# Loads of v on two DMA queues, and three quarters of the E-times-v products summed in f32 before TensorE

## The chip, the core and the metric

The kernel runs on one core of a Trainium2 chip. The metric is device time in microseconds (us): 225.95 us is the median of three runs of the kernel before (225.94 to 226.25). The changed kernel is timed in the same way.

## What is computed

The input x (`A_x`) has 2048 rows of 512 numbers in bf16. After a layernorm it goes through an attention branch and, beside it, through a gated feed-forward branch; their product is added to x:

```python
xn = layernorm(x)
# attention: 32 heads of 16; each position sees w = 0..7, that is position s - 2*w
q, k, v = split(xn @ wqkv)
logits = einsum("bhsd,bhswd->bhsw", q, k[s - 2*w]) * 16 ** -0.5      # s - 2*w < 0 is masked
o = einsum("bhsw,bhswd->bhsd", softmax(logits), v[s - 2*w])
s = o @ wo
# feed-forward
h = gelu_tanh(xn @ w_gate) * (xn @ w_up)                              # 1792 wide
g = silu(h @ w_down)
out = x + s * g
```

## The kernel before

The rows are worked in four chunks of 512 (j = 0 to 3). For each chunk the program issues, in this order:

1. `glu(j, fc)` for fc = 0 to 13 (line 459): eight matmuls give a gate and an up tile in PSUM; ScalarE applies gelu to one (`ge`, line 465) and copies the other (`u`, line 467); VectorE multiplies them into `h` (line 469).
2. `qkv(j + 1, fo)`, twelve projections for the next chunk, each four matmuls and a copy on ScalarE into q, k or v. v goes to DRAM (`vT`, line 290).
3. `down(j, 0)` (14 matmuls into `y_ps`, then silu); then `sums(j)` (line 530); then `down(j, 1..3)`.
4. `divide(j)` (line 449) on VectorE, then `finish(j, 0..3)` (line 488): four matmuls with `wo` into `s_ps`, a product `m` and a sum `o_t` on VectorE, a store.

In chunk 3 there is no next chunk, and `sums(3)` stands before glu fc 12.

Every engine works through its instructions in the order in which the program issues them. What belongs to the attention is put between the stages by hand: `at((stage, j, i), fn, ...)` (line 509) hangs a function on a place, and `run` (line 512) issues it there, ahead of that step's own instructions.

The attention of chunk j lies on VectorE and TensorE:

- `qk_products` (line 320): products of q with k shifted by 2w, 16 instructions, issued in the qkv stage of the chunk before.
- `logits` (line 339): 32 matmuls with a 0/1 matrix sum the products over a head's 16 numbers; ScalarE takes the exponential into `E`. It stands inside `sums` of the chunk before.
- `load_v` (line 300): the array `va` has 128 partitions: partition 32*wl + h holds head h, shifted by 2*wl, with 16 rows of 520 columns. Four DMAs, one for each wl, read it from `vT`. Each fills 32 partitions with 512 runs of 1040 bytes.
- The products of E and v over the four groups g of 4 of the 16 rows, in one of two forms. `av_product` (line 401) takes one group and one half wh of the window: one bf16 product of 2048 columns, twice per group. `av_pair` (line 412) takes one row d of a group and both halves: one product with a result in f32 (`two`), then a sum of the two halves into bf16. It takes four such pairs of instructions for a group, and TensorE then has half as much to sum.
- `av_sums` (line 432): matmuls with 32 output columns sum the products over wl: 4 for each group in the pair form, 8 in the other. [...]

`sums(j)` issues `denominators(j)`, `av_sums(j)`, `logits(j + 1)`, `reciprocals(j)` (VectorE, line 385), the store of the reciprocals to DRAM (line 389), the four loads that spread them (`rb`, line 395), and at last `load_v(j + 1)`. All DMAs are issued by SyncE's queue (SP), in this order.

Buffers that matter: the PSUM pool `mm` has four buffers which are handed out in turn to `g_ps`, `u_ps`, `qkv_ps`, `y_ps`, `s_ps` and the logits; so the first `g_ps` of a chunk takes the buffer of the first `s_ps` of the chunk before, and has to wait until its `m` is done. `ge` and `u` have three buffers each. `va` has one buffer, and half of the next chunk's q-k products (`pk4`) share it.

The loop that sets the places before:

```python
if j + 1 < NJ:
    npair, whole, pairs = 2, (0, 7, 12, 13), (1, 2, 3, 5, 6, 8, 10, 11)
else:
    npair, whole, pairs = 1, (0, 1, 3, 5, 7, 9), (2, 4, 6, 8)
```

`npair` groups are in the pair form; `pairs` and `whole` name the glu steps at which the instructions stand. Chunk 0 has all its groups in the whole form.

Of the kernel before, what the change touches and what calls it, by code (L numbers as in the profile page):

```python
# [18 lines left out]
WL = 4  # L19
# [9 lines left out]
def kernel(  # L29
# [13 lines left out]
    nc = tc.nc  # L43
    B, S, D = A_x.shape
    DF = B_w_gate.shape[1]
    NT, NC, NF, NJ = S // P, D // P, DF // P, S // TQ
# [222 lines left out]
    st = [dict(pk={}, pv={}, vst={}) for _ in range(NJ)]  # L269
# [25 lines left out]
    def qkv(j, fo):  # L295
        ps = mm.tile([P, 1, TQ], F32, name="qkv_ps", tag="mm")
        project(ps[:, 0, :], wqkv_sb, fo * P, j)
        copy_out(j, fo, ps[:])

    def load_v(j, wls=range(WL)):  # L300

        if wls[0] == 0:
            st[j]["va"] = vap.tile([P, DH, VW], BF16, name="v_arr", tag="va")
        va = st[j]["va"]
        for wl in wls:
            nc.sync.dma_start(
                out=va[H * wl : H * (wl + 1), :, :],
                in_=bass.AP(
                    tensor=vT.tensor,
                    offset=PAD + j * TQ - WL * DIL - DIL * wl,  # L310
                    ap=[[SV * DH, H], [SV, DH], [1, VW]],
                ),
            )
# [25 lines left out]
    def logits(j):  # L339
        if j == 0:  # L340
            nc.scalar.preload_act_table(AF.Exp)
            quad = att.tile([P, NC, TQ], F32, name="L_ps", tag="quad")
            L = [quad[:, wh, :] for wh in range(WH)]
        else:
            L = [mm.tile([P, TQ], F32, name="L_ps", tag="mm")[:] for _ in range(WH)]

        Eb = st[j]["Eb"] = ep.tile([P, WH, TQ], BF16, name="E")
        E = st[j]["E"] = Eb[:, ::-1, :]
        for wh in range(WH):
            for c in range(NC):  # L350
                for wl in range(WL):
                    nc.tensor.matmul(  # L352
                        L[wh][H * wl : H * (wl + 1), :],
                        lhsT=dsum[:, c, :],
                        rhs=st[j]["pk"][WL * wh + wl][:, c, :],
                        start=(c == 0),
                        stop=(c == NC - 1),
                    )
        for wh in range(WH):
            nc.scalar.activation(out=E[:, wh, :], in_=L[wh], func=AF.Exp, scale=SCALE)  # L360
        if j == 0:
            for w in range(1, W):
                wh, wl = divmod(w, WL)
                nc.gpsimd.memset(E[H * wl : H * (wl + 1), wh, 0 : w * DIL], 0.0)

    def denominators(j):

        E = st[j]["E"]
        den = mm.tile([P, P], F32, name="den_ps", tag="mm")
        for wh in range(WH):  # L370
            for q in range(4):
                nc.tensor.matmul(  # L372
                    den[H * q : H * (q + 1), :],
                    lhsT=hsum[:],
                    rhs=E[:, wh, q * P : (q + 1) * P],
                    start=(wh == 0),
                    stop=(wh == WH - 1),
                )
        st[j]["den"] = den

    def reciprocals(j):
        den = st[j]["den"]
        rs = sm2.tile([P, P], BF16, name="rs")
        with nc.allow_low_precision(reason="as the softmax of the reference"):
            nc.vector.reciprocal(out=rs[:], in_=den[:])
        st[j]["rs"] = rs

    def store_reciprocals(j):
        nc.sync.dma_start(out=rs_d[j][:, :], in_=st[j]["rs"][:])

    def spread_reciprocals(j):

        rb = op.tile([P, TQ], BF16, name="rb")
        for i in range(WL):
            nc.sync.dma_start(
                out=rb[H * i : H * (i + 1), :].rearrange("h (q i) -> h q i", q=4),
                in_=rs_d[j].rearrange("(q h) i -> h q i", h=H),
            )
        st[j]["rb"] = rb
# [32 lines left out]
    def av_sums(j):  # L432

        o = att.tile([P, NC, TQ], F32, name="o_ps", tag="quad")
        for g in range(NC):
            pv = st[j]["pv"]
            pvs = [pv[g]] if g in pv else [pv[g, wh] for wh in range(WH)]
            for n, p in enumerate(pvs):
                for i in range(4):
                    nc.tensor.matmul(  # L440
                        o[H * i : H * (i + 1), g, :],
                        lhsT=hsum[:],
                        rhs=p[:, i, :],
                        start=(n == 0),
                        stop=(n == len(pvs) - 1),
                    )
        st[j]["o"] = o
# [40 lines left out]
    def finish(j, tt, cols, sl):  # L488

        t, n = j * TPQ + tt, cols.stop - cols.start  # L490
        s = mm.tile([P, n], F32, name="s_ps", tag="mm")
        for g in range(NC):
            nc.tensor.matmul(  # L493
                s[:],
                lhsT=st[j]["oT"][:, g, tt * P : (tt + 1) * P],
                rhs=wo_sb[:, g, cols],
                start=(g == 0),
                stop=(g == NC - 1),
            )
        m = sm2.tile([P, n], BF16, name="m")  # L500
        nc.vector.tensor_tensor(out=m[:], in0=s[:], in1=sl[:], op=ALU.mult)  # L501
        o_t = sm4.tile([P, n], BF16, name="o_t")
        nc.vector.tensor_tensor(out=o_t[:], in0=m[:], in1=x_sb[:, t, cols], op=ALU.add)
        nc.sync.dma_start(out=out2d[t * P : (t + 1) * P, cols], in_=o_t[:])
# [4 lines left out]
    def at(key, fn, *args):  # L509
        side.setdefault(key, []).append((fn, args))  # L510

    def run(stage, j, i):
        for fn, args in side.get((stage, j, i), ()):
            fn(*args)
# [15 lines left out]
    def sums(j):  # L530

        if j + 1 < NJ:
            nc.scalar.preload_act_table(AF.Exp)
        denominators(j)
        av_sums(j)
        if j + 1 < NJ:
            logits(j + 1)
        reciprocals(j)
        store_reciprocals(j)
        spread_reciprocals(j)  # L540
        if j + 1 < NJ:
            load_v(j + 1)

    for j in range(1, NJ):
        at(("qkv", j, 2), k_halo, j)
        for i in range(2):
            at(("qkv", j, 4 + 4 * i), qk_products, j, range(W), 2 * i, 2)

        if j + 1 < NJ:
            npair, whole, pairs = 2, (0, 7, 12, 13), (1, 2, 3, 5, 6, 8, 10, 11)  # L550
        else:
            npair, whole, pairs = 1, (0, 1, 3, 5, 7, 9), (2, 4, 6, 8)
        for i, fc in enumerate(pairs):
            at(("glu", j, fc), av_pair, j, i // 4, i % 4)
        for i, fc in enumerate(whole):
            at(("glu", j, fc), av_product, j, npair + i // 2, i % 2)
    at(("glu", NJ - 1, 12), sums, NJ - 1)

# [3 lines left out]
    pairs = [(8 + 2 * i, mm.tile([P, 2, HQ], F32, name="v_ps", tag="mm")[:]) for i in range(2)]  # L564
# [65 lines left out]
    for n, fo in enumerate((0, 2, 4, 6, 8, 10)):  # L630
# [5 lines left out]
                project(ps[:, i, i0 : i0 + w], wqkv_sb, (fo + i) * P, 0, HQ + i0, w)  # L636
        copy_out(0, fo, ps[:], HQ, HQ, 2)
    at(("glu", 0, 0), transpose_by_dma, TPQ)
    at(("glu", 0, 0), load_v, 0)
    for t in range(TPQ + 1, 2 * TPQ):  # L640
        at(("glu", 0, 0), transpose_by_dma, t)
    at(("glu", 0, 0), load_late_weights)
# [2 lines left out]
    for j in range(NJ):  # L645
        for fc in range(NF):
            run("glu", j, fc)
            glu(j, fc)
        if j + 1 < NJ:

            for i, fo in enumerate((0, 1, 4, 5, 2, 3, 6, 7, 8, 9, 10, 11)):
                run("qkv", j + 1, i)
                qkv(j + 1, fo)
            full = slice(0, D)
            sl = []
            for tt in range(TPQ):
                run("down", j, tt)
                sl.append(down(j, tt, full))
                if tt == 0:
                    sums(j)  # L660
            divide(j)
            for tt in range(TPQ):
                finish(j, tt, full, sl[tt])
        else:
            full, half = slice(0, D), (slice(0, D - P), slice(D - P, D))
            sl = [down(j, tt, full) for tt in range(TPQ - 1)]
            divide(j)
            finish(j, 0, full, sl[0])
            finish(j, 1, full, sl[1])
            finish(j, 2, full, sl[2])  # L670
            sl3 = down(j, 3, half[0])
            finish(j, 3, half[0], sl3)
            sl3 = down(j, 3, half[1])
            finish(j, 3, half[1], sl3)
# [28 lines left out]
```

The softmax here doesn't subtract the row's maximum and nothing guards it: scores larger than these inputs give would overflow.

## Time and profile before

| what | value |
|---|---|
| median of three runs | 225.95 us (225.94 to 226.25) |
| the profiled execution | 226.18 us, of which the span of the profile is 224.5 us |
| TensorE matmul busy | 219.3 us |
| VectorE busy | 172.9 us |
| ScalarE busy | 130.8 us |
| DMA queue | 24.66 MB, 47.1% of 16 engines' span |

The stages of chunk 1 and the start of chunk 2, in us from the span's start, with the busy time of three engines in each stretch:

| stretch | stage | length | TensorE | VectorE | ScalarE |
|---|---|---|---|---|---|
| 72.9 to 97.1 | glu of chunk 1 | 24.20 | 24.09 | 22.36 | 17.08 |
| 97.1 to 107.4 | qkv of chunk 2 | 10.30 | 10.25 | 9.58 | 7.17 |
| 107.4 to 122.9 | down of chunk 1, with the sums | 15.50 | 15.45 | 11.74 | 7.43 |
| 122.9 to 126.3 | finish of chunk 1 | 3.40 | 3.35 | 2.38 | 0.60 |

A chunk thus takes 53.4 us, and the granted clock of TensorE is 1.00 in all of these stretches. In the lines of a profile, a name such as `pv<-E,v_arr` reads "written from"; what stands in brackets at the end of a line of the timeline is the idle time just before it and what ended it.

### The profile page before, as it was taken

What the parts mean: (1) busy time and instruction counts of PE and PEld (TensorE: products, weight loads), DVE (VectorE), ACT (ScalarE), POOL (GpSimd) and SP (SyncE); (2) the same over time, 40 slices, a digit from 0 to 9 for tenths busy, and PEclk for the clock granted to TensorE, in tenths of its full rate; (3) what the DMA queues carried; (4) which work ended last, traced back from release to release, by engine and by line L of the source; (5) the groups of instructions that cost most, each with busy time, mean ns of one, the idle gap of its engine ahead of it and who ended that gap; (6) DMA issues with size and microseconds to landing.
All of it is one profiled execution on the core that took longest, in us unless ns stands there. A gap on an engine that the chain in (4) does not pass through costs nothing.

```text
span 224.5 us, 3548 instructions
## 1 busy us (share of the span) xinstructions
PE 219.3 (98%) x1293; PEld 106.0 (47%) x1314; DVE 172.9 (77%) x295; ACT 130.8 (58%) x207; POOL 21.6 (10%) x67
## 2 busy tenths in 40 slices
PE   8999999999999999999999999999999999999994
PEld 4994444444444444444444444444444444444443
DVE  4688963999984799989984799998944389982452
ACT  4386779667631767676752386767763177666211
POOL 1025981000120000000040000000000000000000
PEclk9999999999999999999999999999999999999999
DMA  6999799972079910000219960000117960001002
GB/s 207 376 402 260 148 198 146 359 212 96 12 152 199 213 23 0 0 3 1 93 41 210 187 164 0 3 0 0 67 41 151 197 147 0 0 0 28 6 23 70
DMA packets 30258, 24.89 MB, mean 111 GB/s; under 512 B 11040, under 2 KB 29728, under 8 KB 30240
## 3 DMA queue, kind: packets, MB, share of 16 engines
q1 hardware_dynamic: 30240, 24.66, 47.1%
q8 instruction: 10, 0.16, 0.3%
q14 instruction: 8, 0.07, 0.1%
HBM read 18.74 MB, written 4.34 MB: 103 GB/s over the span
## 4 chain that ended last, share of the span: by engine, by line
PE 96%; ACT 1%; issue 1%; DVE 0%; ACTq 0%
PE u_ps L261 22%; PE y_ps L477 22%; PE g_ps L261 20%; PE qkv_ps L261 16%; PE s_ps L493 6%; PE L_ps L352 3%; PE o_ps L440 3%; PE qk_ps L576 2%; ACT u L467 1%; PE warm_ps L244 1%; PE v_ps L576 1%; PE qk_ps L567 1%; PE den_ps L372 0%; PE v_ps L567 0%; PE trb L220 0%
## 5 line engine op out<-in xcount | busy, mean ns | idle before, releaser
L261 PE MATMUL u_ps<-xnT,wu_sb 128*128 128x512 bf16 x221 | 57.3, 379 | 0.4
L261 PE MATMUL g_ps<-xnT,wg_sb 128*128 128x512 bf16 x217 | 56.3, 379 | 0.1
L477 PE MATMUL y_ps<-wd_sb,h 128*128 128x512 bf16 (+2 forms) x234 | 49.5, 366 | 0.2
L467 ACT ACTIVATE u<-u_ps 128x512 bf16<-128x512 f32 x56 | 33.5, 599 | 14.8 <-PE u_ps L261 14.8
L465 ACT ACTIVATE ge<-g_ps 128x512 bf16<-128x512 f32 x56 | 33.5, 598 | 11.9 <-PE g_ps L261 8.9
L332 DVE TENSOR_TENSOR pk<-q_sb,k_sb 128x1024 bf16<-128x1024 bf16 (+1 forms) x56 | 38.9, 761 | 1.7 <-ACT k_sb L285 1.7
L261 PE MATMUL qkv_ps<-xnT,wqkv_sb 128*128 128x512 bf16 (+2 forms) x197 | 36.8, 344 | 0.2
L477 PEld LDWEIGHTS <-h 128*128 128x128 bf16 x238 | 22.6, 98 | 26.5 <-issue 1.3
L261 PEld LDWEIGHTS <-wu_sb 128*128 128x128 bf16 x224 | 21.9, 98 | 26.4
L261 PEld LDWEIGHTS <-wg_sb 128*128 128x128 bf16 x224 | 21.7, 98 | 26.6 <-issue 0.8
L404 DVE TENSOR_TENSOR pv<-E,v_arr 128x2048 bf16<-128x2048 bf16 x22 | 26.7, 1220 | 7.4 <-DMA v_arr<-vT 7.4
L485 ACT ACTIVATE sl<-y_ps 128x512 bf16<-128x512 f32 (+2 forms) x17 | 9.7, 572 | 32.7 <-PE y_ps L477 31.6
L469 DVE TENSOR_TENSOR h<-ge,u 128x512 bf16<-128x512 bf16 x56 | 23.1, 419 | 5.9 <-ACT u L467 5.8
L261 PEld LDWEIGHTS <-wqkv_sb 128*128 128x128 bf16 x200 | 18.9, 98 | 17.4
L501 DVE TENSOR_TENSOR m<-s_ps,sl 128x512 bf16<-128x512 f32 (+2 forms) x17 | 11.1, 655 | 18.4 <-PE s_ps L493 13.5
L420 DVE TENSOR_TENSOR two<-E,v_arr 128x1024 f32<-128x1024 bf16 x20 | 24.4, 1218 | 0.0
L204 POOL TENSOR_TENSOR rstd<-rstd,mhalf 128x1 f32<-128x1 f32 x12 | 7.0, 583 | 90.3 <-DVE rstd L201 90.3
L452 DVE TENSOR_TENSOR oT<-o_ps,rb 128x1024 bf16<-128x1024 f32 x8 | 9.4, 1217 | 7.7 <-DMA rb<-rs_d 7.7
L493 PE MATMUL s_ps<-wo_sb,oT 128*128 128x512 bf16 (+2 forms) x64 | 14.6, 366 | 0.2
L428 DVE TENSOR_TENSOR pv<-two 128x512 bf16<-128x512 f32 x20 | 13.8, 692 | 0.7
L465 ACT ACT_TABLE_LOAD x4 | 5.1, 1283 | 11.3 <-PE g_ps L261 11.3
L285 ACT ACTIVATE vst<-qkv_ps 128x512 bf16<-128x512 f32 x14 | 8.4, 597 | 3.7 <-PE qkv_ps L261 3.7
(65 smaller groups left out, 145.2 us busy)
## 6 DMA issues: line engine op xcount, KB each, us to landing
v_arr<-vT SPq DMA_DIRECT2D x16, 520.0 KB, 8.5
vT<-vst SPq DMA_DIRECT2D x8, 256.0 KB, 2.4
out_dram<-o_t SPq DMA_DIRECT2D x15, 128.0 KB, 3.4
wg_sb<-in_B_w_gate_dram SPq DMA_DIRECT2D x2, 896.0 KB, 9.9
wu_sb<-in_B_w_up_dram SPq DMA_DIRECT2D x2, 896.0 KB, 11.2
wd_sb<-in_B_w_down_dram SPq DMA_DIRECT2D x1, 1792.0 KB, 11.6
wqkv_sb<-in_A_wqkv_dram SPq DMA_DIRECT2D x4, 384.0 KB, 4.4
x_sb<-in_A_x_dram SPq DMA_DIRECT2D x3, 512.0 KB, 7.8
```

The costliest lines, as they stand in the source:

```text
L261: nc.tensor.matmul(ps, lhsT=w[:, dk, lo : lo + P], rhs=xnT[j][:, dk, i0 : i0 + n], start=(dk == 0), stop=(dk == NC - 1),)
L332: nc.vector.tensor_tensor(out=st[j]["pk"][w][:, c0 : c0 + n, :], in0=st[j]["q"][:, c0 : c0 + n, :], in1=k_sb[j][:, c0 : c0 + n, off : off ...
L404: nc.vector.tensor_tensor(out=pv[:], in0=st[j]["E"][:, wh, :].unsqueeze(1).to_broadcast([P, 4, TQ]), in1=st[j]["va"][:, 4 * g : 4 * g + 4, ...
L420: nc.vector.tensor_tensor(out=two[:], in0=st[j]["Eb"][:], in1=bass.AP(tensor=v.tensor, offset=v.offset, ap=[v.ap[0], [WL * DIL, WH], [1, T ...
L428: nc.vector.tensor_tensor(out=st[j]["pv"][g][:, d, :], in0=two[:, 0, :], in1=two[:, 1, :], op=ALU.add)
L465: nc.scalar.activation(out=ge[:], in_=g_ps[:], func=AF.Gelu_apprx_tanh)
L467: nc.scalar.activation(out=u[:], in_=u_ps[:], func=AF.Copy)
L469: nc.vector.tensor_tensor(out=h[:], in0=ge[:], in1=u[:], op=ALU.mult)
L477: nc.tensor.matmul(y[:], lhsT=st[j][fc][:, tt * P : (tt + 1) * P], rhs=wd_sb[:, fc, cols], start=(fc == 0), stop=(fc == NF - 1),)
L485: nc.scalar.activation(out=sl[:], in_=y[:], func=AF.Silu)
L493: nc.tensor.matmul(s[:], lhsT=st[j]["oT"][:, g, tt * P : (tt + 1) * P], rhs=wo_sb[:, g, cols], start=(g == 0), stop=(g == NC - 1),)
L501: nc.vector.tensor_tensor(out=m[:], in0=s[:], in1=sl[:], op=ALU.mult)
```

## The change

Three things change.

1. `load_v` takes a queue. The loads of wl 0 and 1 (partitions 0 to 63) stay on SyncE's queue, those of wl 2 and 3 (partitions 64 to 127) are issued by ScalarE's queue. In `sums` they stand on ScalarE behind the two exponentials; for chunk 0 they stand at glu step 4.
2. In chunks 1 and 2 three groups of four take the pair form (two before), in chunk 3 two (one before).
3. The places move: the first `av_pair` of chunk j stands at the start of `finish(j - 1, 0)`, that is on VectorE between the `divide` and the first `m`; in chunks 1 and 2 the last two pairs stand at the first step of the qkv stage; and `sums(3)` stands before glu fc 13 and not 12.

```diff
-    def load_v(j, wls=range(WL)):
-
-        if wls[0] == 0:
+    def load_v(j, wls, queue):
+
+        if "va" not in st[j]:
             st[j]["va"] = vap.tile([P, DH, VW], BF16, name="v_arr", tag="va")
         va = st[j]["va"]
         for wl in wls:
-            nc.sync.dma_start(
+            queue.dma_start(
...
         if j + 1 < NJ:
-            load_v(j + 1)
+
+            load_v(j + 1, (0, 1), nc.sync)
+            load_v(j + 1, (2, 3), nc.scalar)
...
         if j + 1 < NJ:
-            npair, whole, pairs = 2, (0, 7, 12, 13), (1, 2, 3, 5, 6, 8, 10, 11)
+            npair, whole, pairs = 3, (4, 9), (0, 1, 2, 3, 6, 7, 8, 11, 12, 14, 14)
         else:
-            npair, whole, pairs = 1, (0, 1, 3, 5, 7, 9), (2, 4, 6, 8)
+            npair, whole, pairs = 2, (3, 6, 9, 11), (0, 1, 2, 4, 5, 7, 8)
+        at(("finish", j - 1, 0), av_pair, j, 0, 0)
         for i, fc in enumerate(pairs):
-            at(("glu", j, fc), av_pair, j, i // 4, i % 4)
+            key = ("glu", j, fc) if fc < NF else ("qkv", j + 1, 0)
+            at(key, av_pair, j, (i + 1) // 4, (i + 1) % 4)
         for i, fc in enumerate(whole):
             at(("glu", j, fc), av_product, j, npair + i // 2, i % 2)
-    at(("glu", NJ - 1, 12), sums, NJ - 1)
+    at(("glu", NJ - 1, 13), sums, NJ - 1)
...
-    at(("glu", 0, 0), load_v, 0)
+    at(("glu", 0, 0), load_v, 0, (0, 1), nc.sync)
+    at(("glu", 0, 4), load_v, 0, (2, 3), nc.scalar)
...
             for tt in range(TPQ):
+                run("finish", j, tt)
                 finish(j, tt, full, sl[tt])
```

## The prediction

> **What bounds the kernel now.** I read the page's busy times first, then the chain of waits, then VectorE's and SyncE's timelines over one chunk, then the DMA lines of the v loads.
>
> ```profile
> PE 219.3 (98%) x1293; PEld 106.0 (47%) x1314; DVE 172.9 (77%) x295; ACT 130.8 (58%) x207; POOL 21.6 (10%) x67
> ```
>
> TensorE is busy for 219.3 of 224.5 us: it hardly ever waits. Only matmuls taken away can shorten the time, and any new wait of TensorE adds to it. The chain has the sums of products that the change touches:
>
> ```profile
> 110.69 1.29 PE o_ps L440 x24
> ```
>
> 24 of them take 1.29 us, 54 ns each. The instructions on VectorE, from the groups by line:
>
> ```profile
> L404 DVE TENSOR_TENSOR pv<-E,v_arr 128x2048 bf16<-128x2048 bf16 x22 | 26.7, 1220 | 7.4 <-DMA v_arr<-vT 7.4
> L420 DVE TENSOR_TENSOR two<-E,v_arr 128x1024 f32<-128x1024 bf16 x20 | 24.4, 1218 | 0.0
> L428 DVE TENSOR_TENSOR pv<-two 128x512 bf16<-128x512 f32 x20 | 13.8, 692 | 0.7
> ```
>
> VectorE's timeline around the end of chunk 1 (start, length, instruction, idle time before and who ended it):
>
> ```profile
> 110.85 0.95 DVE L385 RECIPROCAL rs<-den_ps 128x128 bf16<-128x128 f32 x1
> ...
> 117.78 2.36 DVE L452 TENSOR_TENSOR oT<-o_ps,rb 128x1024 bf16<-128x1024 f32 x2 [0.72 <-DMA rb<-rs_d]
> 123.86 0.69 DVE L501 TENSOR_TENSOR m<-s_ps,sl 128x512 bf16<-128x512 f32 x1 [3.72 <-PE s_ps L493]
> ...
> 129.44 1.23 DVE L404 TENSOR_TENSOR pv<-E,v_arr 128x2048 bf16<-128x2048 bf16 x1 [1.26 <-DMA v_arr<-vT]
> ```
>
> See that VectorE has a hole of 3.72 us ahead of the first `m`, and that v lands only at 129.44, 5.6 us after that `m`. The queue that issues the loads:
>
> ```profile
> 111.82 0.33 SPq L389 DMA_DIRECT2D rs_d<-rs  x1
> 113.30 2.66 SPq L395 DMA_DIRECT2D rb<-rs_d  x4
> 116.14 2.70 SPq L306 DMA_DIRECT2D v_arr<-vT  x4
> ```
>
> The first v load goes out 4.34 us after the reciprocal has ended (111.80). In the other chunks this step is 3.41 us (58.90 to 62.31) and 3.87 us (165.22 to 169.09). The second and fourth load of chunk 2, each looked up alone, land so many us after their own issue (last column):
>
> ```profile
> v_arr<-vT SPq DMA_DIRECT2D x1, 520.0 KB, 7.3
> v_arr<-vT SPq DMA_DIRECT2D x1, 520.0 KB, 11.2
> ```
>
> The second is issued 0.68 us after the first, so half of v is there 8.0 us after the first issue (8.2 and 8.1 us in the other chunks), all of it after 13.3.
>
> [...] bandwidth from 65 to 78 us, 40 slices:
>
> ```profile
> GB/s 243 208 176 176 186 195 189 198 195 195 173 202 182 246 234 214 198 202 202 176 233 189 186 170 179 198 179 181 181 191 158 59 20 42 359 394 369 397 278 281
> ```
>
> It stays near 190, rises to 246 at 69.2 us, 1.3 us before the second load lands (70.5), where the queue passes from partition 63 to 64, and is 359 to 397 for rows over all 128 partitions. So both halves side by side should take about half as long. [...] No run here shows two issuers[...]. [...]
>
> **The change part by part.**
>
> *TensorE.* Each of chunks 1, 2 and 3 loses four sums: 12 x 54 ns = 0.65 us less.
>
> *VectorE.* A group changes from 2 x 1.14 us (start to next start) to four pairs of 1.86 us (77.74 to 79.00 and 0.60 more): 7.44 - 2.28 = 5.2 us more a chunk. With its `h`, a pair takes 2.20 us (79.94 to 82.14) and a whole one 1.475 us (184.02 to 185.49); an `h` alone 0.34. The glu stage of chunks 1 and 2 gets 9 x 2.20 + 2 x 1.475 + 3 x 0.34 = 23.8 us (24.2 before, 129.44 to 153.6), the qkv stage 2 x 1.86 = 3.7 us, the hole before `m` 1.86 us.
>
> *ScalarE.* Two issues at 0.66 us (2.65 us for four on SP) = 1.3 us, behind the exponentials. Those end at 60.94, the next silu waits for TensorE with 1.21 us to spare, and its PSUM buffer is wanted four tiles later: cost 0, and 0 up to 3 us. In chunk 0 they stand at about 24.7 us, v being stored by 22.57 (when SP went on): gelu is late by 1.3 us where two PSUM tiles allow 1.7. What is behind them, gelu and the copies, loses no more: 0.
>
> *The new wait.* The first pair of chunk j needs all of v and stands ahead of `m`. Behind it are the four `m`, and TensorE's next four PSUM tiles wait for those. Before, the last `m` ended at 74.30 and its buffer was wanted at 75.34; less 0.1 for the signal there is 0.95 us of room. And a late reciprocal makes the wait longer, as SP issues wl 0 and 1 behind `rb`. That closes a loop on VectorE, from one reciprocal's end to the next:
>
> - to the first v issue 3.9 us (mean of the three above);
> - to the landing of SP's half 8.0 us. ScalarE's half starts earlier (114.4 in chunk 2) and is not last;
> - first pair 1.86; four `m` and `o_t` 4 x 1.06 = 4.24 (123.86 to 124.92);
> - glu 23.8; two pairs 3.7; sixteen q-k products 9.67 (9.72 to the reciprocal's place); reciprocal 0.95.
>
> The sum is 56.1 us. Before, the same loop was 4.34 + 13.3 + 24.2 + 9.65 + 0.95 = 52.4 us, and 0.97 us of waiting for k made it TensorE's 53.4. Now it is longer than TensorE's period of 53.4 - 0.2, and VectorE with its DMAs sets the pace over the chunk ends.
>
> The times: chunk 0's v lands at 30.6 (SP, 22.57 + 8.0) and 32.7 (ScalarE, 24.7 + 8.0), before VectorE wants it at 33.8, so its 3.75 us of waiting goes and the products q-k start when k is copied, 47.3 in place of 48.31. First reciprocal: 58.90 - 0.9 = 58.0. The next ones: 114.1 and 170.2. The first `m` comes 3.9 + 8.0 + 1.86 = 13.76 us later: 71.8, 127.9, 184.0, against 70.43, 123.86, 177.28 before. After the third, TensorE is late by 184.0 - 177.28 - 0.95 = 5.8 us (0.4 at the first end, then about 2.7 at each; the savings of chunks 1 and 2 are in it).
>
> *Chunk 3.* VectorE leaves the last `o_t` at 188.2; up to the product at step 11 it has 7 x 2.20 + 3 x 1.475 + 0.34 + 1.14 = 21.3 us: 209.5. TensorE enters the glu at 179.76 + 5.8, and 13 steps of 1.73 us, 0.23 and 20 sums later (209.3) it wants that product: 0.4 us of waiting, less 0.2 saved. The later reciprocal (about 211.2) gives `oT` at 211.2 + 6.1 + 2.4 = 219.7; TensorE's three downs last to 220.6: covered.
>
> Sum: 5.8 + 0.4 - 0.2 = 6.0 us on the profiled execution's 226.18, that is 232.2, and 232.0 on the median of 225.95.
>
> *Unknown costs.* The issue step: 3.4 to 4.3 us. SP's landing: [...] up to 9.2 if both streams hinder each other or `rb` and its store. Each us of the two together counts three times: 3.9 + 8.0 give 232, 11.0 together 229, 13.5 together 237. I take the measured values, since nothing in the trace says which way sharing goes.
>
> **Rivals.**
>
> - *The cover holds, faster.* If issue and landing together take at most 10.0 us (two us less, over three ends, cancels the 5.8), no `m` is late and the 0.65 us remain: 225.3. For it: VectorE's hole is 3.7 us wide and the pair 1.86. Against it: SP's half alone needs 8.0.
> - *No bandwidth is gained.* [...] all 2048 runs take their 12 us from ScalarE's first: 60.94 + 1.2 + 12 + 1.3 = 75.4, first `m` at 77.3, 5.9 us too late, and about as much at each end, since the loads follow the exponentials: 3 x 5.8 + 0.2 = 17.6, that is 243.5. [...] against it: the step to 246.
> - *Half the lateness.* Between 10.0 and 11.0 us together: 225.5 to 228.5.
>
> **Numbers.** About 0.2% (0.45 us) can be told from no change here. Likeliest, 228.5 to 237: 0.72. Half: 0.08. Cover holds: 0.11. No bandwidth: 0.06. Over 237 otherwise: 0.03. The range 226.5 to 237.5 takes in the likeliest and most of the half. Faster 0.11, same 0.03, slower 0.86.
>
> **What would show it.** SP's half landing 8 us after its first issue and bandwidth over 300 GB/s; VectorE idle about 4 us on v ahead of a first pair; `g_ps` waiting for `m` at the chunk ends, most at the second and third; reciprocals 56 us apart; 96 sums in place of 108. I am wrong if reciprocals stay 53.4 us apart, or if v is there before VectorE leaves `divide`.

## The result and the profile after

| | kernel before | changed kernel |
|---|---|---|
| median of six runs | 226.12 us (225.94 to 226.68) | 241.69 us (241.40 to 242.22) |
| ratio to the kernel before | 1 | 1.069, 95% interval 1.067 to 1.071 |
| profiled execution, its span | 226.18, 224.5 us | 242.10, 240.4 us |
| reciprocals of chunks 0, 1, 2 end at | 58.90, 111.80, 165.22 | 61.10, 119.33, 177.98 |
| first `m` at the end of chunks 0, 1, 2 starts at | 70.43, 123.86, 177.28 | 76.94, 135.59, 193.82 |

The change costs 15.6 us where 6.0 were predicted. The direction was right, the size was outside the range. A single execution that took over 1.5% longer than the fastest of its kernel (there is one in each of two experiments below) is left out of the times.

First the page of the changed kernel: busy times, the granted clock in 40 slices, and the two DMA queues (q1 is SyncE's, q10 ScalarE's: packets, MB, share of 16 engines' time).

```profile
PE 225.0 (94%) x1281; PEld 105.8 (44%) x1302; DVE 187.6 (78%) x313; ACT 129.9 (54%) x207; POOL 20.9 (9%) x67
...
PEclk9999999999997999999999899999999999999999
...
q1 hardware_dynamic: 26016, 20.40, 33.1%
q10 hardware_dynamic: 4224, 4.26, 10.0%
```

TensorE has 1281 matmuls in the records in place of 1293, the twelve sums fewer, and yet 15.4 us in which it does nothing (240.4 - 225.0), against 5.2 before. Its busy time has grown as well, from 219.3 to 225.0 us: the `s_ps` matmuls take 18.0 us in place of 14.6, some of them at a lower clock (last section). VectorE has 14.7 us more, about what the pairs cost (three times 5.2 us was predicted). The 4.26 MB of q10 are ScalarE's halves of v: four times 1.065 MB.

Where the new idle time is can be read from the waits of the changed kernel (us in total, times, longest):

```profile
DVE oT L452 <- DMA rb<-rs_d: 22.3, 4, 9.6
...
PE s_ps L493 <- DVE oT L452: 6.9, 6, 2.1
...
DVE two L420 <- DMA v_arr<-vT: 4.0, 2, 2.0
```

In the kernel before, the first of these lines was

```profile
DVE oT L452 <- DMA rb<-rs_d: 7.7, 3, 5.3
```

The wait that has grown most is one that the prediction did not have: `oT`, the product of `divide`, waits for `rb`, the spread reciprocals. The expected wait of a first pair (`two`) for v is there but looks small, since `oT` in front of it has already used up most of the time. TensorE in turn waits 6.9 us at `s_ps` for `oT`. VectorE's timeline at the end of chunk 1:

```profile
118.38 0.95 DVE L385 RECIPROCAL rs<-den_ps 128x128 bf16<-128x128 f32 x1
129.39 2.35 DVE L452 TENSOR_TENSOR oT<-o_ps,rb 128x1024 bf16<-128x1024 f32 x2 [4.79 <-DMA rb<-rs_d]
133.72 1.23 DVE L420 TENSOR_TENSOR two<-E,v_arr 128x1024 f32<-128x1024 bf16 x1 [1.98 <-DMA v_arr<-vT]
...
135.59 0.68 DVE L501 TENSOR_TENSOR m<-s_ps,sl 128x512 bf16<-128x512 f32 x1
```

Here `oT` starts at 129.39 (117.78 before), the first pair at 133.72, the first `m` at 135.59. Now the DMA issues of the same stretch, first ScalarE's, then SyncE's:

```profile
119.38 1.23 ACTq L306 DMA_DIRECT2D v_arr<-vT  x2
```

```profile
119.36 0.33 SPq L389 DMA_DIRECT2D rs_d<-rs  x1
123.21 1.75 SPq L395 DMA_DIRECT2D rb<-rs_d  x4
125.08 1.28 SPq L306 DMA_DIRECT2D v_arr<-vT  x2
```

ScalarE sends its half (119.38) with its last exponential, which starts at 119.15. The store of the reciprocals goes out at the same moment and SyncE can go on 3.85 us later (1.5 us before: 111.82 to 113.30). This is so at this end alone: at the two others SyncE goes on after 1.5 us. ScalarE's half is not shown to be the reason, for in two runs below (all loads by turns on one queue, and ScalarE's half later) the store takes 3.1 and 3.4 us at this end with no load of v under way. Then come `rb` and at last SyncE's half. What the loads do meanwhile is in the DMA view of chunk 0's end. Over 61 to 76 us, 40 slices:

```profile
GB/s 0 0 74 13 69 189 230 322 241 191 191 193 193 186 204 198 200 183 189 243 298 261 208 194 189 191 197 186 197 189 186 197 182 183 180 115 51 0 0 0
```

Apart from two short steps, at the start of the loads and at the passage from ScalarE's to SyncE's, the bandwidth stays near 190 GB/s until both halves are in: this is the line of the kernel before again, with no long part in which the halves run side by side. The queues in 64.5 to 67.5 us, while both have work (SyncE issues `rb` from 62.59 on):

```profile
q10 hardware_dynamic: 572, 0.58, 110.8%
q1 hardware_dynamic: 42, 0.01, 2.7%
```

and in 69 to 73 us:

```profile
q1 hardware_dynamic: 771, 0.79, 113.3%
```

So in these windows the queues are served one after the other: ScalarE's half has 572 of the 614 packets of the first, SyncE's all 771 of the second. What SyncE issues later waits, `rb` included. The line of one `rb` load of this end (KB, us to landing):

```profile
rb<-rs_d SPq DMA_DIRECT2D x1, 32.0 KB, 6.9
```

For 32 KB that took 1.9 us before. v is whole at 74.9 us, 13.7 us after ScalarE's first issue at 61.20 (14.1 and 13.7 us at the other ends). Before, it was whole 13.2 to 13.9 us after the first of four issues on one queue. Nothing has been gained.

### The profile page after: what moved, and what is told of

It is laid out like the page before. It is cut to its first block, busy times and chain, and to the rows that moved or that the text cites. A ratio compares the mean times of both kernels' runs of the same rounds, so it can differ in the third digit from the quotient of the medians.

```text
span 240.4 us, 3539 instructions
## 1 busy us (share of the span) xinstructions
PE 225.0 (94%) x1281; PEld 105.8 (44%) x1302; DVE 187.6 (78%) x313; ACT 129.9 (54%) x207; POOL 20.9 (9%) x67
## 3 DMA queue, kind: packets, MB, share of 16 engines
q10 hardware_dynamic: 4224, 4.26, 10.0%
## 4 chain that ended last, share of the span: by engine, by line
DVE 55%; PE 19%; DMA 18%; issue 4%; SPq 2%; ACTq 0%; DVEq 0%; ACT 0%
DMA v_arr<-vT 17%; DVE two L420 15%; DVE pk L332 12%; DVE pv L428 9%; PE y_ps L477 8%; DVE pv L404 7%; DVE h L469 6%; DVE m L501 3%; PE qkv_ps L261 2%; PE g_ps L261 2%; PE u_ps L261 2%; PE qk_ps L580 1%; SPq L395 1%; PE s_ps L493 1%; DMA rs_d<-rs 1%
## 5 line engine op out<-in xcount | busy, mean ns | idle before, releaser
L420 DVE TENSOR_TENSOR two<-E,v_arr 128x1024 f32<-128x1024 bf16 x32 | 39.0, 1219 | 6.1 <-DMA v_arr<-vT 4.0
L467 ACT ACTIVATE u<-u_ps 128x512 bf16<-128x512 f32 x56 | 33.4, 596 | 10.8 <-PE u_ps L261 10.0
L493 PE MATMUL s_ps<-wo_sb,oT 128*128 128x512 bf16 (+2 forms) x64 | 18.0, 420 | 7.2 <-DVE oT L452 6.9
L404 DVE TENSOR_TENSOR pv<-E,v_arr 128x2048 bf16<-128x2048 bf16 x16 | 19.3, 1218 | 6.1 <-DMA v_arr<-vT 6.1
L428 DVE TENSOR_TENSOR pv<-two 128x512 bf16<-128x512 f32 x32 | 22.1, 692 | 1.1
L493 PEld LDWEIGHTS <-oT 128*128 128x128 bf16 x68 | 6.8, 109 | 18.0 <-DVE oT L452 9.8
```

The costliest lines, as they stand in the source:

```text
L404: nc.vector.tensor_tensor(out=pv[:], in0=st[j]["E"][:, wh, :].unsqueeze(1).to_broadcast([P, 4, TQ]), in1=st[j]["va"][:, 4 * g : 4 * g + 4, ...
L420: nc.vector.tensor_tensor(out=two[:], in0=st[j]["Eb"][:], in1=bass.AP(tensor=v.tensor, offset=v.offset, ap=[v.ap[0], [WL * DIL, WH], [1, T ...
L428: nc.vector.tensor_tensor(out=st[j]["pv"][g][:, d, :], in0=two[:, 0, :], in1=two[:, 1, :], op=ALU.add)
L467: nc.scalar.activation(out=u[:], in_=u_ps[:], func=AF.Copy)
L493: nc.tensor.matmul(s[:], lhsT=st[j]["oT"][:, g, tt * P : (tt + 1) * P], rhs=wo_sb[:, g, cols], start=(g == 0), stop=(g == NC - 1),)
```

## The experiments

All times are medians, with ratios to the kernel before of the same series (226.2 us). "Theory S" in the expectations is the reading just given: queues are served one after the other, so that the ScalarE half delays `rb` and then SyncE's half. Diffs are against the changed kernel unless it is said otherwise.

**The two parts apart.** First the loads on two queues alone, with the places and pairs of the kernel before (diff against that):

```diff
-            load_v(j + 1)
+            load_v(j + 1, (0, 1), nc.sync)
+            load_v(j + 1, (2, 3), nc.scalar)
...
```

> The kernel before with only the split of the v loads over two queues. Theory S (the two queues are served one after the other in the order of issue, and the loads that spread the reciprocals stand behind ScalarE's half of v): rb lands some 5 us later than before at each of three chunk ends, oT then misses TensorE by about 2.5 us each time, and nothing is gained on v: 231 to 236 us; the whole of v lands no sooner than 1.5 us ahead of before. Theory P (halves overlap [...], and only the small loads are hindered): rb is late too, but the last v load lands 4 us or more sooner than before after its first issue; 229 to 234 us.

Measured: 237.38 us, ratio 1.052 (1.048 to 1.056). The loads alone, with no new arithmetic, cost 11.2 us, more than either theory had. In what was to tell the theories apart, the whole of v, it is theory S: v is whole 13.5 to 13.8 us after the first issue, no sooner than before. VectorE's timeline of this run at the end of chunk 1:

```profile
116.54 0.95 DVE L385 RECIPROCAL rs<-den_ps 128x128 bf16<-128x128 f32 x1
127.88 2.35 DVE L452 TENSOR_TENSOR oT<-o_ps,rb 128x1024 bf16<-128x1024 f32 x2 [5.13 <-issue]
131.01 0.69 DVE L501 TENSOR_TENSOR m<-s_ps,sl 128x512 bf16<-128x512 f32 x1 [0.77 <-PE s_ps L493]
132.88 0.69 DVE L501 TENSOR_TENSOR m<-s_ps,sl 128x512 bf16<-128x512 f32 x1 [0.72 <-PE s_ps L493]
```

`oT` comes 10.4 us after the reciprocal's end (117.49); before it was 6.0 us (111.80 to 117.78). The idle time in front of it is put down to "issue" at this end, but the last `rb` lands at 127.7, just ahead of `oT`; at the two others it is put down to `rb` (4.22 and 10.07 us). The four `rb` loads of this end differ by what was issued before them: the first two, issued before ScalarE's first load (119.69), land 1.8 and 2.0 us after their issue; the third and the fourth, issued behind its first and its second load, take 4.5 and 7.1 us.

A second cost shows too: the first two `m` are 1.87 us apart and not 1.07, since TensorE's second `s_ps` waits for the first `m` here (0.85 us at each end, 2.6 us in all), as if it had been handed the PSUM buffer of the first one. At the first end the clock was low as well (0.83 in 72 to 76 us, 0.75 in 76 to 80). So not all of the 11.2 us is the lateness of `rb`, and the theories had only that.

Then the places and pairs alone, all loads on SyncE:

```diff
-            load_v(j + 1, (0, 1), nc.sync)
-            load_v(j + 1, (2, 3), nc.scalar)
+            load_v(j + 1, range(WL), nc.sync)
...
-    at(("glu", 0, 0), load_v, 0, (0, 1), nc.sync)
-    at(("glu", 0, 4), load_v, 0, (2, 3), nc.scalar)
+    at(("glu", 0, 0), load_v, 0, range(WL), nc.sync)
```

> The changed kernel with all v loads on SyncE's queue again, so only the places and the pair form are changed. The loop on VectorE (first issue 3.9 us behind the reciprocal, v 13.4 us later, then 44.2 us of VectorE's work) is 61.5 us from reciprocal to reciprocal: reciprocals end at about 58.9, 120.4 and 181.9, the last first m comes at 201, and the time is about 249 us. If the split of the queues is what costs, it is below the changed kernel's 241.7; if the places cost and the split helps, above it.

Measured: 250.0 us, ratio 1.105 (1.102 to 1.107). Its timeline, end of chunk 1:

```profile
126.27 2.36 DVE L452 TENSOR_TENSOR oT<-o_ps,rb 128x1024 bf16<-128x1024 f32 x2 [0.55 <-DMA rb<-rs_d]
137.79 1.22 DVE L420 TENSOR_TENSOR two<-E,v_arr 128x1024 f32<-128x1024 bf16 x1 [9.17 <-DMA v_arr<-vT]
```

This is the loop of the prediction in its pure form: `rb` in time, and a first pair that waits 9.17 us for v. The first `m`, issued behind that pair, starts at 139.66, as the pair ends. Reciprocals are 61.7 us apart, the first `m` at the end of chunk 2 at 201.04 where 201 was expected. So the loop's arithmetic holds, and the two parts don't add up (11.2 and 23.8 give 35, together they cost 15.6): in these places the second queue does help, since ScalarE's issue comes 3.3 us ahead of SyncE's (61.20 against 64.51), with no spreading in front of it: from the reciprocal to the first pair it is 17.0 us at the first end with one queue and 14.0 with two.

**ScalarE's half behind `rb`.** If the half that is issued first delays `rb`, a later issue must bring `rb` back:

```diff
-            load_v(j + 1, (2, 3), nc.scalar)
...
                 if tt == 0:
                     sums(j)
+                if tt == 1:
+                    load_v(j + 1, (2, 3), nc.scalar)
```

> The changed kernel with ScalarE's half of v issued behind the silu of down(j, 1), some 3 us later, so that the rb loads go first. Both theories: rb lands 2 us after its issue and oT is in time. Theory S: ScalarE's half follows SyncE's, v is whole about 13.4 us after SyncE's first issue, the loop is 61 us: 247 to 252 us. Theory P: the halves overlap, v is whole 9 to 10 us after SyncE's first issue, bandwidth over 300 GB/s for some us, the loop 57.6 us: 236 to 241 us.

Measured: 249.04 us, ratio 1.102 (1.099 to 1.105), in the range of theory S. At the ends of chunks 0 and 2 `rb` landed in time (`oT` at 66.11, the changed kernel 70.74). At the end of chunk 1 ScalarE's first load went out at 125.77, ahead of the last `rb` (126.25), and that one load took 5.2 us where the other three took 1.6 to 1.8. v was whole only at 76.7, though the two halves were issued at the same time here (64.34 and 64.44). The DMA view of this run shows something else in 71 to 73.5 us:

```profile
DMA packets 788, 0.81 MB, mean 324 GB/s; under 512 B 28, under 2 KB 787, under 8 KB 787
...
q1 hardware_dynamic: 415, 0.42, 55.9%
q10 hardware_dynamic: 372, 0.37, 50.9%
```

When a load of each half does run at the same time, 324 GB/s go through, and not 190. The prediction's estimate from the bandwidth before, about half the time with both halves side by side, is thus not far off for such a stretch. What failed is that the queues seldom have both halves under way at once.

**The halves by turns on one queue.** This should have both halves under way without a second queue: eight loads of eight rows each on SyncE, alternating between partitions 0 to 63 and 64 to 127. The diff is against the kernel with all loads on SyncE (250.0 us).

```diff
-        for wl in wls:
+        for wl, d in ((0, 0), (2, 0), (0, 8), (2, 8), (1, 0), (3, 0), (1, 8), (3, 8)):
             queue.dma_start(
-                out=va[H * wl : H * (wl + 1), :, :],
+                out=va[H * wl : H * (wl + 1), d : d + 8, :],
...
```

> The changed kernel with v loaded on SyncE's queue alone, in eight DMAs of 8 rows that go by turns to partitions 0 to 63 and 64 to 127. Theory P: [...] turns on one queue bring most of what two queues would: v whole 8 to 10 us after the first issue, bandwidth 250 GB/s or more between, 231 to 238 us. Theory S alone [...]: v takes 12 to 14 us as before, and the time is that of the places alone, about 249 us.

Measured: 238.49 us, ratio 1.052 (1.048 to 1.057). The first pair starts 9.3 us after the first issue (61.80 to 71.14), in place of 13.6 (62.23 to 75.84). But v is not whole then. The pair reads row 0 alone, and rows 0 to 7 are in with the sixth of the eight pieces. The lines of the sixth and of the last piece, issued at 64.13 and 65.11:

```profile
v_arr<-vT SPq DMA_DIRECT2D x1, 260.0 KB, 6.9
v_arr<-vT SPq DMA_DIRECT2D x1, 260.0 KB, 8.8
```

v is whole at 73.9, 12.1 us after the first issue (11.5 and 11.8 us at the other ends; 13.3 to 13.4 us with the four whole loads). So the run changes two things at once. The turns bring 1.3 to 1.8 us. The larger part, 2.3 to 2.9 us, comes from cutting the loads along the rows, so that the first pair need not wait for all of v; a run with that cut and no turns was not made. Where later expectations have v whole after 9.3 us, this start of the first pair is meant. The bandwidth over 61 to 76 us is mostly between 200 and 250 GB/s while v is read:

```profile
GB/s 44 70 85 84 42 153 308 314 244 247 194 183 266 230 214 241 216 211 225 236 205 216 244 200 219 250 241 205 231 183 181 144 21 18 4 0 0 172 178 0
```

It is still slower than the kernel before, since v is issued only after the reciprocals, their store and `rb`, and the loop runs over all of these.

The same pieces on two queues, ScalarE's behind the silu of `down(j, 1)`, chunk 0 on SyncE alone (against the changed kernel):

```diff
-            load_v(j + 1, (2, 3), nc.scalar)
...
+                if tt == 1:
+                    load_v(j + 1, (2, 3), nc.scalar)
...
+        for wl, d in [(wl, d) for a in (0, 1) for d in (0, 8) for wl in wls if wl % 2 == a]:
...
```

> The places of the changed kernel; SyncE issues its half of v in four DMAs of 8 rows, ScalarE the other half in four behind the silu of down(j, 1), chunk 0 all on SyncE in turns. If two queues run side by side once the pieces are small, 300 GB/s or more for most of the load, v whole 8 to 9 us after SyncE's first issue, 233 to 237 us. If the queues are still served one DMA after the other, no better than the turns on one queue, 238 to 242 us.

Measured: 241.24 us, ratio 1.067 (1.063 to 1.071). The ends differ. At the end of chunk 0 ScalarE issues (63.97) when all four of SyncE's pieces have been issued. Its pieces land after SyncE's, at about 190 GB/s again, and v is whole 14.1 us after the first issue. At the two other ends ScalarE's first issue (123.17) falls between SyncE's (from 122.64 on). There the pieces of the two queues land by turns, and v is whole after 10.7 and 11.3 us. In 124 to 132 us:

```profile
DMA packets 2251, 2.09 MB, mean 261 GB/s; under 512 B 295, under 2 KB 2250, under 8 KB 2250
...
q1 hardware_dynamic: 1216, 1.06, 55.9%
q10 hardware_dynamic: 1034, 1.02, 54.4%
```

So the small pieces of two queues did mix where they were issued by turns. The time is no better than with turns on one queue all the same; the reciprocals on either side of the first end are 60.3 us apart, those on either side of the second 57.6.

**Chunk 0.** In the changed kernel its v was late as well (ScalarE's half landed at 35.7 and 39.6 us, all of v at 37.4 before), and the first reciprocal ended at 61.1 where 58.0 was predicted. Does that count?

```diff
-    at(("glu", 0, 0), load_v, 0, (0, 1), nc.sync)
-    at(("glu", 0, 4), load_v, 0, (2, 3), nc.scalar)
+    at(("glu", 0, 0), load_v, 0, range(WL), nc.sync)
```

> The changed kernel with chunk 0's four loads on SyncE's queue, as before; the other chunks keep two queues. Theory: ScalarE's half of chunk 0, which stood among the transposes and weights, made the first reciprocal 3.1 us late, and every later one with it. Then the first reciprocal ends at about 58.9 in place of 61.1, and the time falls by 2 to 3 us against the changed kernel, to 238.5 to 240. Rival: the loop on VectorE catches up that start anyway, no change from 241.7.

Measured: 242.06 us, ratio 1.069 (1.066 to 1.073): no change. The reciprocal ended at 58.74, 2.4 us earlier, the first `m` came only 0.6 us earlier (76.35). SyncE's half was issued 2.4 us earlier, at 62.09, and was in only at 74.3, 12.2 us later: an earlier issue behind ScalarE's half brings next to nothing. v follows ScalarE's issue, which comes with the last exponential (61.20 in the changed kernel, 60.93 here), and not the reciprocal.

**The first pair behind the `m`.** 

```diff
-        at(("finish", j - 1, 0), av_pair, j, 0, 0)
+        at(("glu", j, 0), av_pair, j, 0, 0)
```

> The changed kernel with the first pair issued at glu step 0, behind the four m and o_t. Theory A (what costs is that the m wait for v): the m come when s_ps is there, and nearly all of the loss is gone, 230 us or less. Theory B (the loop from reciprocal to reciprocal is too long for VectorE, wherever the pair stands): oT still waits for rb, the loop shrinks by only 1 to 1.5 us each time, 236 to 240 us.

Measured: 245.51 us, ratio 1.085 (1.080 to 1.089). Both theories fell: it is 4 us slower than the changed kernel. `rb` was late as ever (`oT` at 70.40, 129.70 and 189.71), so the `m` were late without the pair in front of them, and the pair's 1.86 us no longer lay in that hole; reciprocals were 59.1 and 60.1 us apart. How the rest of the 4 us divides between the PSUM buffers (again the second `s_ps` waited 0.85 us for the first `m`) and the lower clock of TensorE (0.82 in 72 to 76 us, 0.75 in 76 to 80) was not separated.

**The reciprocals out of the loop.** If the loop over reciprocal, store, `rb` and v is the cause, v must be issued without waiting for them. The denominators need only `E`, which is there a chunk earlier. The diff is against the kernel with eight loads by turns on SyncE:

```diff
     def sums(j):
-        denominators(j)
         av_sums(j)
         if j + 1 < NJ:
             logits(j + 1)
-        reciprocals(j)
-        store_reciprocals(j)
-        spread_reciprocals(j)
...
+    def early(j):
+        denominators(j)
+        reciprocals(j)
+        store_reciprocals(j)
+        spread_reciprocals(j)
+
+    for j in range(NJ):
+        at(("glu", j, 5 if j else 13), early, j)
```

> The turns on one queue, with the denominators, reciprocals, their store and the rb loads moved from the sums into the glu stage (step 5; step 13 for chunk 0), and v issued right behind the logits. Theory: the leg of 3.9 us from reciprocal to first issue leaves the loop; it is then 1.6 + 9.3 + 44.2 = 55 us from the end of the q-k products to the next, against 53.2 for TensorE, about 2 us late at two of three ends: 227.5 to 231 us. Rival: the late landing of v as such (9 us) is what costs, and the time stays over 235.

Measured: 229.74 us, ratio 1.016 (1.014 to 1.017). Of the 15.6 us, 12 are gone, with the pairs and the places of the change kept. The first `m` stand at 71.81, 126.81 and 180.83. TensorE hardly waits at the chunk ends (`g_ps` for an `m` once, 0.2 us); VectorE waits for v three times, 15.0 us in all, in holes where it had waited for `s_ps` before (4.00 and 3.72 us at the first two).

Two more runs start from here. With the kernel before's own places and pairs:

```diff
-            npair, whole, pairs = 3, (4, 9), (0, 1, 2, 3, 6, 7, 8, 11, 12, 14, 14)
+            npair, whole, pairs = 2, (0, 7, 12, 13), (1, 2, 3, 5, 6, 8, 10, 11)
...
-        at(("finish", j - 1, 0), av_pair, j, 0, 0)
...
```

> The kernel before with its own places and its own number of pairs, but loads of v by turns on one queue and early reciprocals. It shows what the loads alone are worth when they cost nothing else. VectorE's first product of a chunk stands behind the m here and TensorE is busy 98%, so a faster v should bring nothing: 225.5 to 227, no difference from the kernel before. If it does, the 3.6 us by which the same loads with the changed places stand above the kernel before belong to the places alone. The rival, that the denominators in the glu stage or the eight loads cost TensorE something, gives 228 or more.

Measured: 227.05 us, ratio 1.004 (1.002 to 1.005), 0.8 us slower than the kernel before. So the loads and early reciprocals cost 0.8 us by themselves, and 2.7 of the 3.5 us belong to the places: even where the first pair can start 9.2 to 10.2 us after the first issue of v, v comes a little late for a pair ahead of `m`. No variant beat the kernel before.

With the two-queue loads of the changed kernel, both halves now issued at the same moment:

```diff
-            load_v(j + 1, range(WL), nc.sync)
+            load_v(j + 1, (0, 1), nc.sync)
+            load_v(j + 1, (2, 3), nc.scalar)
```

> The loads of the changed kernel (SyncE wl 0 and 1, ScalarE wl 2 and 3, whole rows), but reciprocals, their store and their spreading are done in the glu stage, so that SyncE issues its half right behind the logits, within about 0.5 us of ScalarE's, and no small load stands between. Only the overlap of the two queues is asked. If two queues work side by side when both are issued at once, v is whole about 8 us after the first issue, the first m of chunk 1 is at about 70.5 and the time is 226 to 229. If the queues are served one after the other even then, v is whole 12.5 to 13.5 us after the first issue, 3 to 4 us later than with loads by turns on one queue (9.3, time 229.7); times three chunk ends that is 239 to 242.

Measured: 238.21 us, ratio 1.054 (1.048 to 1.059), a little under the serial forecast. Neither picture is quite right, as the DMA view of the last chunk shows. The loads go out at 176.47 (SyncE) and 176.69 (ScalarE). In 180 to 183 us:

```profile
DMA packets 621, 0.63 MB, mean 208 GB/s; under 512 B 20, under 2 KB 621, under 8 KB 621
...
q10 hardware_dynamic: 482, 0.50, 87.1%
q1 hardware_dynamic: 139, 0.13, 25.3%
```

and in 183 to 186 us:

```profile
DMA packets 995, 1.00 MB, mean 333 GB/s; under 512 B 34, under 2 KB 995, under 8 KB 995
...
q10 hardware_dynamic: 524, 0.53, 56.6%
q1 hardware_dynamic: 471, 0.47, 51.1%
```

The first load of each queue goes almost alone, SyncE's and then ScalarE's; only the second loads run side by side. The first pair starts 10.8 us after the first issue here, 12.3 us in the other two chunks, where the last packets straggle. So early reciprocals bring 3.5 us with these loads and loads by turns bring 3.2 us without early reciprocals (238.49), but both together bring 12.0. There are two delays, the step from the reciprocal to the issue of v and the time from there to the first pair, and as long as one of them stands, it sets the end.

Last, `rb` on a third queue in the changed kernel, GpSimd's:

```diff
         for i in range(WL):
-            nc.sync.dma_start(
+            nc.gpsimd.dma_start(
                 out=rb[H * i : H * (i + 1), :].rearrange("h (q i) -> h q i", q=4),
```

> The changed kernel with the four small loads of the reciprocals (rb) issued by GpSimd in place of SyncE; SyncE then issues its half of v right behind the store of the reciprocals, 1.7 us earlier. If a load waits because it is issued later than ScalarE's half, on whatever queue, rb lands again 5 us or more after its issue and oT of chunk 0 starts at 70 or later; v is whole 13.5 us after ScalarE's first issue all the same, and the time stays at 240 to 243. If only SyncE's queue is held back, rb lands 2 to 3 us after its issue, oT starts at about 66, but v stays the last of the first pair's inputs: 239 to 242. If the earlier issue of SyncE's half makes the two halves overlap, v is whole at 72 or earlier and the time falls to 232 to 236.

Measured: 240.48 us, ratio 1.061 (1.054 to 1.067). GpSimd's issue and VectorE's timeline of this run:

```profile
62.22 2.36 POOL L395 DMA_DIRECT2D rb<-rs_d  x4 [25.61 <-DMA rs_d<-rs]
```

```profile
70.45 2.36 DVE L452 TENSOR_TENSOR oT<-o_ps,rb 128x1024 bf16<-128x1024 f32 x2 [3.29 <-DMA rb<-rs_d]
72.72 1.22 DVE L420 TENSOR_TENSOR two<-E,v_arr 128x1024 f32<-128x1024 bf16 x1
```

`rb` is as late as before (6.6 us from issue to landing), so it isn't SyncE's queue that holds it: in 62.0 to 64.2 us, with ScalarE's half issued first (60.59), 459 of 464 packets are ScalarE's, 5 SyncE's and none GpSimd's. And v, whose halves were issued 0.4 us apart, is whole 11.5 us after the first issue (13.0 and 12.0 us at the other ends, where 13.5 was expected), by the time `oT` is done: the first pair starts without a wait. One delay has gone and the other stands in its place, with the same time in the end. In this run `rb` alone was enough to keep the loop at its length.

## Why the prediction was wrong in size

In its own steps:

- **TensorE's 0.65 us**: the twelve sums are gone (96 are left), 54 ns each in the trace before (24 in 1.29 us, where four full matmuls take 0.86 us, 216 ns each). They count nothing while TensorE waits.
- **VectorE's prices**: right. A pair with its `h` takes 2.20 us (81.18 to 83.38); the glu stage 23.71 us (81.18 to 104.89; predicted 23.8); the two pairs in qkv 3.86 (3.7); the q-k products 9.63 (9.67).
- **ScalarE's issues**: 1.23 us for two (predicted 1.3), hidden as predicted: its next silu waits for TensorE all the same (0.62 to 0.68 us at the three ends).
- **Chunk 0**: wrong, and without weight. Predicted were 30.6 and 32.7 us for v and 58.0 for the reciprocal; ScalarE's half came at 39.6, behind SyncE's half and among the transposes. Undoing it changed nothing.
- **The new wait**: the loop is the right one, and this term of it failed: "to the landing of SP's half 8.0 us. ScalarE's half starts earlier (114.4 in chunk 2) and is not last". An early start of ScalarE's half was booked as harmless. It is what makes SyncE's half last: that lands 10.4, 8.4 and 10.4 us after its first issue, because ScalarE's half is served first (572 packets to 42). At the second end the issue itself is 5.75 us behind the reciprocal (3.9 predicted); the store took 3.85 us there, and what held it is open. From the reciprocal to the first pair it is 13.97, 14.39 and 13.97 us in place of 11.9.

The loop of chunk 1 by measured terms is 13.97 + 1.87 (pair) + 4.24 (`m` and `o_t`) + 23.71 + 3.86 + 9.63 + 0.95 = 58.23 us, which is the distance of the reciprocals (61.10 to 119.33); predicted were 56.1. The excess at the three ends is 2.07 + 2.49 + 2.07 us, and the first reciprocal was 3.1 us late, together 9.7: the third first `m` came at 193.82 and not 184.0, and the profiled execution took 242.1 and not 232.2 us. The 3.1 us are booked here by the place in the timeline; the run with chunk 0's loads undone shows that v is bound to the exponentials, so they would not have been saved.

- **Chunk 3**: predicted 0.4 us of waiting for the late product; it was 0.53.
- **What would show it**: reciprocals 56 us apart and over 300 GB/s were named, and both failed to appear (58.2 and 58.7 us, 190 GB/s), which points to the failed term directly. `g_ps` waiting for `m` was to be the main stall; it waits 1.4 us once, and starts 0.05 us after that `m` (194.50 to 194.55; 0.1 was allowed for the signal). TensorE stood earlier, at `s_ps`, for `oT`.
- **The rivals**: "No bandwidth is gained" gave v 14.5 us after ScalarE's first issue and 243.5 us; 13.7 to 14.1 and 241.7 were measured. For this kernel its number was nearly right, but not because no more can go through: both halves at once do reach 324 to 333 GB/s. The loads just weren't under way at once. The prediction gave this rival a chance of 0.06. The bandwidth before (190 GB/s for one half, 359 to 397 for rows over all 128 partitions) gave an estimate of what two halves can pass together; that two queues would have them under way together was the author's assumption, and no run had shown it. In this kernel a second issuer alone made nothing faster (237.38 us), and its packets did not mix with those of the first (572 against 42), save for the small pieces issued by turns (1216 against 1034) and for second loads (524 against 471).

Also for `rb` no cost was considered: it was four small loads that had taken 1.9 us, ahead of SyncE's half in its own queue. The bound "up to 9.2 if both streams hinder each other or `rb` and its store" named it, but only as a part of SyncE's landing, and not as the wait in front of `divide`.

What stays open: why the later queue gets so little while an earlier load is under way (42 of 614 packets), and why, of two whole loads on each of two queues, only the second ones overlap (208 GB/s, then 333). The traces show when packets moved, and not what decides it.

## What to carry to other kernels

Here a second DMA queue was no second path (v whole after 13.7 to 14.1 us, 13.2 to 13.9 before). So before a large load moves to one, ask what is issued after that load on any queue, and price a small load behind it at the rest of the large one (here 6.9 us in place of 1.9). If two halves of the partitions are to be filled at once, issue short loads by turns and look at the bandwidth line for the step up (here from 190 to 261 GB/s on two queues); and cut them so that what the first instruction reads comes first, which brought more here (2.3 to 2.9 us against 1.3 to 1.8). And where a wait closes a loop over several chunks, look for everything that ends within a few us of it: shortening either of the two delays here brought 3.2 or 3.5 of 15.6 us, shortening both brought 12.

## What was unexpected in the hardware

- One queue's packets kept another's almost out for 3 us (572 to 42), and small loads waited behind it on SyncE's queue and on GpSimd's alike (6.9 and 6.6 us). Two loads into different halves of the partitions ran one after the other as well (208 GB/s, 482 packets to 139), until each queue was at its second load (333 GB/s). Pieces of 260 KB that two queues issued by turns did run mixed (261 GB/s).
- TensorE's clock fell after short stalls, at two of three ends. In the changed kernel TensorE stands still from 70.4 to 72.0 us and again for 0.53 us, and then the windows show (us, busy us of PE, PEld, DVE, ACT and POOL, granted clock, DMA share, GB/s):

```profile
70.00:72.00 2.00, 0.38 (x2) 0.00 (x0) 1.26 (x2) 0.60 (x1) 0.00 (x0) 1.00 1.13 191
72.00:74.00 2.00, 1.45 (x5) 0.41 (x6) 1.10 (x1) 0.00 (x0) 0.00 (x0) 0.79 1.16 187
74.00:76.00 2.00, 2.00 (x6) 0.74 (x5) 0.93 (x1) 0.00 (x0) 0.00 (x0) 0.50 0.39 42
76.00:78.00 2.00, 1.78 (x8) 0.85 (x8) 1.93 (x4) 0.00 (x0) 0.00 (x0) 0.86 0.00 0
```

From 73.3 to 76.6 us the granted clock is 0.50, after 1.65 and 0.53 us of standing still. The second end shows the same (2.06 and 0.53 us, then 0.50 from 131.3 to 134.6). At the third end 1.58 and 0.52 us left the clock at 1.00, and so did 2.00 and 0.53 us at the first end of the run with `rb` on GpSimd; the length of these stalls alone does not decide it, and what does was not shown. The lower clock doesn't explain the time: over the six runs of the changed kernel the mean clock lay between 0.979 and 1.000 and the time between 241.4 and 242.2 us, and the run with 1.000 was the slowest one. The slow matmuls lie where VectorE's first pair and `m` are what the chunk waits for.
